# Sums of squares, and the ones that add them, in bf16; the totals of q, k and v half a step later

## The chip, the cores and the metric

The kernel runs on one core of a Trainium2 chip. The metric is the time of one execution on the device in microseconds, the median over several runs. In the text PE is TensorE, PEld its weight loads, DVE is VectorE, ACT is ScalarE, POOL is GpSimd and SP is SyncE, which issues most transfers.

## The reference

Attention with a block-causal mask, a gated two-layer network, and a routed layer of eight experts, one after the other:

```python
scores = np.where(mask, q @ k.T / 8, -1e9)      # 8 batches x 8 heads, 576 x 576, d = 64
x = softmax(scores) @ v                         # 4608 tokens x 512
x = ((x @ w1) * (x @ w2) @ w3) @ w_out          # 512 -> 1024 -> 512
# moe2: logits = x @ w_gate; greedy assignment of 4608 tokens to 8 experts of 576 places
out[mask_e] = np.maximum(x[mask_e] @ ew1[e], 0) @ ew2[e]
```

Everything is float32 in the reference.

## The kernel before, in words

A float32 operand is split into two f16 halves, a high and a low one, and a product is three f16 products (high x high, high x low, low x high). For this each operand is first scaled by a power of two that brings it to the middle of the f16 range. The power comes from a sum of squares: `ssq` (L200) lets ACT square a tile and accumulate one sum per partition in a small tile (`qm`, `vm`, `wm`, `w3m`, `wom`, `wgxm`, `wgym`), and `total` (L139) lets PE multiply a 128x128 matrix of ones with these columns, which adds them over the partitions and puts the total on each of them (L145). The product lies in one of three PSUM buffers `ab`, which the gated network also uses. DVE reads it in `pow2` (L74) and makes the power of two and its inverse with integer shifts; only the exponent of the total matters. `split` (L181) then lets ACT make the high half (L188) and DVE the low half (L183).

The work is in three stages. The first, up to about 690 us, runs attention and the gated layer together. It is cut into 64 half steps (two heads of one batch, one part of their rows), numbered h; each half step has, in this order on PE, the attention output of an earlier half step (PV, L431), the scores of the next one (S, L328 and L332, in part L392) and two units of the gated layer (L464: 12 products with `w1h`, 12 with `w2h`, then the gate product on DVE, L480, stored as g). Beside it the weights are decoded from their 64-bit form, split, and w3 and w_out multiplied together (L723, L736, `w34o`). The second stage makes the output of the network (L1152) while DVE assigns the tokens to experts. The third, from about 1054 us, runs the experts (L1344, L1362); their weights are split in `expert_w`, with totals at L1230.

Each piece of the first stage is an event with a place on a time scale of half steps: `at(p, f)` puts f at place p, `defer(d, f)` at d after the present one, and the program is written in the order of the places. `spread` looks for a free slot behind the exponentials or the gate products. Up to half step 14, some 190 us, a planner of the framework then orders all engines by its own estimate of times; from there on PE keeps the written order, and the planner orders ACT, DVE, SP and POOL alone. In the third stage PE, ACT and DVE keep the written order.

Lines that the change touches: the tile `ones` (L66) and the two masks made from it (L68, L754); `scale_v` (L218), which asks for the squares of v of a batch from place 8b - 1.4 on and for the total .55 after the last of them (L239); `qk_scale` (L264), which handles q and k of two pairs of heads as a group, with the total d1 after the second square (L274), d1 = .62 for the groups from number 6 on; and the tiles of sums elsewhere.

Of the kernel before, what the change touches and what calls it, by code (L numbers as in the profile page):

```python
# [8 lines left out]
F32 = mybir.dt.float32  # L9
F32R = mybir.dt.float32r  # L10
F16 = mybir.dt.float16
BF16 = mybir.dt.bfloat16
I32 = mybir.dt.int32
AF = mybir.ActivationFunctionType
ALU = mybir.AluOpType
# [40 lines left out]
def moe_kernel(ctx, tc, q, k, v, moe_w1, moe_w2, moe_w3, moe_w_out, w_gate, ew1, ew2, out):  # L56
    nc = tc.nc
    P = 128
# [3 lines left out]
    const = ctx.enter_context(tc.tile_pool(name="const", bufs=1))  # L62
    L = const.tile([P, NT, E], F32, name="L")
    ident = const.tile([P, P], F32, name="ident")
    i8 = const.tile([P, 8], F32, name="i8")
    ones = const.tile([P, P], F32, name="ones")  # L66
    nc.gpsimd.memset(ones, 1.0)
    nc.gpsimd.affine_select(out=ident, in_=ones, pattern=[[1, P]], compare_op=ALU.is_equal, fill=0.0,  # L68
                            base=0, channel_multiplier=-1)

    id16 = const.tile([P, P], F16, name="id16")
# [21 lines left out]
    sm = pa.enter_context(tc.tile_pool(name="sm", bufs=4))  # L93
# [21 lines left out]
    def at(p, f, *a):  # L115
        assert p >= now[0], (p, now[0])
        heapq.heappush(ev, (p, at.n, f, a))
        at.n += 1
# [3 lines left out]
    def defer(d, f, *a):  # L122
        at(now[0] + d, f, *a)
# [74 lines left out]
    sc_c, iv, sv, ivs = {}, {}, {}, {}  # L198

    def ssq(x, dst, junk):  # L200
        nc.scalar.activation(junk, x, AF.Square, accum_out=dst)

    def load_qk(g):
        n0, n1 = GROUPS[g]
# [11 lines left out]
        nc.sync.dma_start(v32, v[b])  # L216

    def scale_v(b):  # L218
        m = sm.tile([P, 3], F32, name="vm")
        vhl[4 * b] = c2.tile([P, 2, 2, 5, D], F16, name="v16", bufs=4)  # L220
        j = vhl[4 * b].rearrange("p z h j d -> p (z h j d)")

        def sq(x):
            w = min(2, 5 - 2 * x)
            ssq(v32[:, :, 2 * x:2 * x + w, :], m[:, x:x + 1],
                j[:, :H * w * D].rearrange("p (h j d) -> p h j d", h=H, j=w))

        def use(m2):
            m3 = sm.tile([P, 1], F32, name="vm3")
            nc.vector.tensor_reduce(m3, m2, axis=AX.X, op=ALU.add)  # L230
            sv[b] = pow2(sm, m3, "vp")

        for x in range(3):
            if b:
                p = spread("a", now[0] + .1 * x, sq, x)
            else:
                behind("e", sq, x)
                p = now[0] - .15
        at(p + .55, total, m, .08, use)  # L239

    def prep_v(n):
        b, hp = divmod(n, NP)
# [18 lines left out]
    pq = {}  # L261

    junk = c2.tile([P, 2, S], F16, name="junk", bufs=1)

    def qk_scale(g, d0, d1, d2):
        n0, n1 = GROUPS[g]
        w = n1 - n0

        def sq(z):
            if z == 0:  # L270
                pq[g] = sm.tile([P, 2], F32, name="qm")
            ssq(qk32[g][:, z, :w], pq[g][:, z:z + 1], junk)
            if z:
                defer(d1, total, pq[g], .08, fin)  # L274

        def fin(m2):
            T = c2.tile([P, 2, 2, 2, S], F16, name="qkT")
            s, e = pow2(sm, m2, "qp")
            c = sm.tile([P, 2], F32, name="cc")
            for z, f in enumerate((1.0, -1.0)):  # L280
                nc.vector.scalar_tensor_tensor(c[:, z:z + 1], e[:, 0:1], f * 0.125, e[:, 1:2],
                                               op0=ALU.mult, op1=ALU.mult)
            for z in range(2):
                split(T[:, z, 0, :w], T[:, z, 1, :w], qk32[g][:, z, :w], s[:, z:z + 1], .14,
                      then=lambda: end(d2), key="g5" if g == 4 else "g")
            pq[g] = s, c, T

        done = []

        def end(_):  # L290
            done.append(1)
            if len(done) < 2:
                return
            s, c, T = pq.pop(g)
            del qk32[g]
            for n in range(n0, n1):
                qkT[n] = T[:, 0, :, n - n0], T[:, 1, :, n - n0], q4[:, n % 2], c
            if g + 2 < len(GROUPS):
                load_qk(g + 2)

        if g == 4:
            defer(0, behind, "e", sq, 0)
            defer(.02, behind, "e", sq, 1)
            return
        spread("a", now[0], sq, 0)
        spread("a", now[0] + d0, sq, 1)

# [290 lines left out]
    def prep_w(f):  # L598
        w = stg_w.tile([P, 1024], F32, name="wd")
        t = [w16[n][f].rearrange("p z c f -> p z (c f)") for n in ("w1", "w2")]  # L600

        def use(m2):
            s, e = pow2(sm, m2, "wp")
            nc.vector.scalar_tensor_tensor(iw12[:, f:f + 1], e[:, 0:1], 2.0 ** 15, e[:, 1:2], op0=ALU.mult,
                                           op1=ALU.mult)
            for z in range(2):
                split(t[z][:, 0], t[z][:, 1], w[:, 512 * z:512 * z + 512], s[:, z:z + 1], .08)

        def squares():
            m = sm.tile([P, 2], F32, name="wm")  # L610
            for z in range(2):
                ssq(w[:, 512 * z:512 * z + 512], m[:, z:z + 1], t[z][:, 1])
            defer(.5, total, m, .06, use)

        decode(("w", f), w, squares)
# [4 lines left out]
    wo = {}  # L620

    def wo_chunk(c):
        if c == 0:
            es_w.close()
            wo["s2"] = es_g.enter_context(tc.tile_pool(name="stg_2", bufs=1))
            st_o = wo["stack"] = ExitStack()
            wo["pool"] = st_o.enter_context(tc.tile_pool(name="stg_o", bufs=1))
            wo["w"] = wo["pool"].tile([P, 8, 512], F32, name="wo32")
            wo["m"] = sm.tile([P, 8], F32, name="wom", bufs=1)
            wo["t"] = wo["s2"].tile([P, 8, 2, 512], F16, name="wo16", bufs=1)  # L630
            wo["g"] = wo["s2"].tile([P, 4 * E], F32, name="wg", bufs=1)
            nc.scalar.dma_start(wo["g"].rearrange("p (c e) -> p c e", e=E),
                                w_gate.rearrange("(c p) e -> p c e", p=P))
        decode(("o", c), wo["w"][:, c], lambda: ssq(wo["w"][:, c], wo["m"][:, c:c + 1], wo["t"][:, c, 1]))

    def hilo(src, k, name, then):
        m = sm.tile([P, 1], F32, name=name + "m", bufs=1)
        t = wo["s2"].tile([P, k, 2, E], F16, name=name + "h", bufs=1)
        v = src.rearrange("p (c e) -> p c e", e=E)
        ssq(v, m, t[:, :, 1])  # L640

        def use(m2):
            s, e = pow2(sm, m2, name + "p")
            split(t[:, :, 0], t[:, :, 1], v, s, .05)
            defer(.06, then, t, e)

        defer(.4, total, m, .05, use)
# [48 lines left out]
    def w3_chunk(f, h):  # L696
        if h == 0:
            wo["w3"] = wo["p3"].tile([P, 1024], F32, name="w3d", bufs=1)
        w3 = wo["w3"]

        def use(m2):
            t = wo["T", f]
            s, e = pow2(sm, m2, "w3p")
            split(t[:, 0], t[:, 1], w3, s, .12, then=lambda: wo.update({("ok", f): True}))
            fc = sm.tile([P, 2], F32, name="w3f")
            nc.vector.tensor_tensor(out=fc[:, 0:1], in0=e, in1=wo["e"], op=ALU.mult)
            nc.vector.tensor_tensor(out=fc[:, 1:2], in0=e, in1=wo["ee"], op=ALU.mult)
            wo["T", f] = t.rearrange("p z (k f) -> p z k f", f=P), fc

        def squares():  # L710
            m = sm.tile([P, 1], F32, name="w3m")
            wo["T", f] = wo["p3"].tile([P, 2, 1024], F16, name="w3h", bufs=2)
            at(spread("a", now[0], ssq, w3, m, wo["T", f][:, 1]) + .55, total, m, .06, use)

        decode(("3", f, h), w3[:, h * 512:h * 512 + 512], squares if h else lambda: None)
# [35 lines left out]
    i8b = const.tile([P, 8], F32, name="i8b")  # L751
    for x in range(4):
        t = i8b if x else i8
        nc.gpsimd.affine_select(out=t, in_=ones[:, :8], pattern=[[1, 8]], compare_op=ALU.is_equal, fill=0.0,  # L754
                                base=32 * x, channel_multiplier=-1)
        if x:
            nc.vector.tensor_tensor(out=i8, in0=i8, in1=i8b, op=ALU.add)
# [451 lines left out]
    def expert_w(e, part):  # L1209
# [3 lines left out]
        d = {}  # L1213
# [4 lines left out]

        def red(i):
            if i == 0:  # L1220
                d["m"] = cw.tile([P, 8], F32, name="em" + n, bufs=2)
                d["w"] = cw.tile([P, 2, A_, N_], F16, name="ew" + n, bufs=2)
                d["s"] = d["st"].rearrange("p c f -> p (c f)")
                d["v"] = d["w"].rearrange("p z c f -> p z (c f)")
            nc.scalar.activation(d["v"][:, 1, i * width:(i + 1) * width], d["s"][:, i * width:(i + 1) * width], AF.Square,  # L1225
                                 accum_out=d["m"][:, i:i + 1])

        def fin():
            m2 = cwp["ps"].tile([P, 512], F32, name="pe")
# [203 lines left out]
```

## Time and profile before

| | |
|---|---|
| median of 3 runs | 1443.48 us (1442.46 to 1443.8) |
| the profiled execution | 1445.88 us |
| its span in the profile | 1444.2 us |
| PE busy | 1319.5 us, 91% |
| DVE, ACT busy | 965.2 us, 952.5 us |
| mean granted clock of PE | 0.964 |

The profile is one execution. The span runs from the first to the last instruction; some 1.7 us lie around it. A row of a timeline gives start, duration, engine, line, operation and shapes, with a count where like instructions are merged, and in brackets how long the engine stood idle before it and who released it. A duration of merged products of PE runs to the end of the last one and overlaps the next row. The granted clock is 1.00 at 2.4 GHz and 0.50 at 1.2 GHz; a value between is a mean over time at the two levels.

### The profile page before, as it was taken

The numbers are of one execution on the slowest core, as the hardware profiler recorded it, in microseconds if no ns is written. First come the engines' busy times: TensorE is split into PE (matmuls) and PEld (weight loads), VectorE is DVE, ScalarE is ACT, GpSimd is POOL, SyncE is SP. The second block draws the span as 40 slices with busy tenths as digits, with TensorE's granted clock in tenths as the row PEclk, the third lists the DMA queues.
The fourth block names the chain that finished last, engine by engine and source line by source line (L and its number), as shares of the span: only waits on it lengthen the run. The fifth ranks groups of instructions, "written<-read, shape, count | busy, mean of one in ns | idle before, by whom it ended". The sixth has DMA issues, their size and how long they took to land. (4 is left out here: it accounts for less than half of the span.)

```text
span 1444.2 us, 31983 instructions
## 1 busy us (share of the span) xinstructions
PE 1319.5 (91%) x12483; PEld 909.6 (63%) x12483; DVE 965.2 (67%) x2873; ACT 952.5 (66%) x2229; POOL 114.2 (8%) x136
## 2 busy tenths in 40 slices
PE   4678889879999999999999899999889999999997
PEld 3455567657766666666676566666576566666663
DVE  7997878887988978787514677777454456354530
ACT  7896788968888888777534465455346667675641
POOL 0000000000000000010001110111032211110001
PEclk6789999999999999999999999999989999999999
DMA  9776878598977787599999978888585785665200
GB/s 291 196 180 182 196 169 176 136 194 189 190 180 157 185 190 175 137 199 246 237 286 242 224 183 199 199 212 202 148 155 141 159 199 145 174 161 155 74 30 37
DMA packets 383815, 257.47 MB, mean 178 GB/s; under 512 B 260784, under 2 KB 344752, under 8 KB 382640
## 3 DMA queue, kind: packets, MB, share of 16 engines
q1 hardware_dynamic: 370464, 213.44, 60.2%
q0 software_dynamic: 11520, 39.87, 12.5%
q10 hardware_dynamic: 1680, 2.11, 0.5%
q8 instruction: 98, 1.61, 0.5%
q14 instruction: 53, 0.43, 0.1%
HBM read 130.84 MB, written 39.86 MB: 118 GB/s over the span
## 5 line engine op out<-in xcount | busy, mean ns | idle before, releaser
L464 PE MATMUL ab<-xT,w1h 128*128 128x288 f16 x1536 | 215.6, 290 | 15.5 <-ACT a_sb L474 6.0
L464 PE MATMUL ab<-xT,w2h 128*128 128x288 f16 x1536 | 214.9, 290 | 9.6 <-ACT a_sb L474 6.7
L1344 PE MATMUL pe<-xT,ewa 128*128 128x288 f16 (+2 forms) x1728 | 193.4, 275 | 1.6 <-ACT xT L1312 0.9
L1362 PE MATMUL pe<-ewb,h 128*128 128x512 f16 (+1 forms) x960 | 189.3, 379 | 0.0
L464 PEld LDWEIGHTS <-w1h 128*128 128x128 f16 x1536 | 147.7, 100 | 60.6 <-issue 18.9
L464 PEld LDWEIGHTS <-w2h 128*128 128x128 f16 x1536 | 151.8, 99 | 53.5 <-issue 12.5
L1344 PEld LDWEIGHTS <-ewa 128*128 128x128 f16 x1728 | 158.1, 100 | 36.1 <-issue 2.0
L374 DVE SCALAR_TENSOR_TENSOR P<-E,rr,P 128x128 f16<-128x128 f32 (+4 forms) x288 | 154.5, 574 | 25.7 <-ACT P L370 22.1
L354 ACT ACTIVATE E<-S,nb,cc 128x384 f32<-128x384 f32 (+4 forms) x234 | 147.8, 640 | 2.1
L1362 PEld LDWEIGHTS <-h 128*128 128x128 f16 (+1 forms) x960 | 85.4, 101 | 98.8 <-issue 2.6
L370 ACT ACTIVATE P<-E,rr 128x384 f16<-128x384 f32 (+2 forms) x224 | 120.5, 602 | 19.2 <-issue 7.9
L1152 PE MATMUL px<-W34h,gl 128*128 128x512 f32 x288 | 120.6, 419 | 3.9 <-DMA gl<-g 3.9
L1152 PE MATMUL px<-W34h,gh 128*128 128x512 f32 x288 | 120.9, 420 | 0.8 <-ACT gh L1173 0.8
L1152 PE MATMUL px<-W34l,gh 128*128 128x512 f32 x288 | 120.3, 418 | 0.0
L431 PE MATMUL PV<-PT,v 128*64 128x128 f16 (+1 forms) x2880 | 90.1, 218 | 13.3 <-DMA PT<-P 13.0
L346 DVE TENSOR_REDUCE nb<-S 128x2 f32<-128x768 f32 (+3 forms) x128 | 100.0, 815 | 3.0 <-PE S L332 2.7
L431 PEld LDWEIGHTS <-v 128*64 128x64 f16 x2880 | 77.9, 114 | 33.1 <-issue 27.7
L1347 DVE SCALAR_TENSOR_TENSOR h<-pe,h 128x288 f16<-128x288 f32 (+2 forms) x144 | 57.8, 420 | 47.2 <-ACT h L1346 46.3
L1365 ACT ACTIVATE y<-pe,s 128x512 f32<-128x512 f32 x36 | 24.7, 687 | 95.0 <-PE pe L1362 65.8
L1302 DVE SCALAR_TENSOR_TENSOR x<-xg,xsc,x 128x512 f16<-128x512 f32 x36 | 27.1, 752 | 84.0 <-ACT x L1301 84.0
L1346 ACT ACTIVATE h<-pe 128x288 f16<-128x288 f32 (+2 forms) x144 | 52.6, 376 | 44.9 <-PE pe L1344 42.0
L1187 ACT ACTIVATE jk<-px 128x512 f16<-128x512 f32 x36 | 21.4, 595 | 89.9 <-issue 67.4
(298 smaller groups left out, 2266.9 us busy)
## 6 DMA issues: line engine op xcount, KB each, us to landing
g<-gd SPq DMA_DIRECT2D x36, 512.0 KB, 5.1
gl<-g POOLq DMA_DIRECT2D x36, 512.0 KB, 5.5
raw<-in_moe_w_dram SPq DMA_DIRECT2D x32, 512.0 KB, 4.5
esa<-in_moe_w_dram SPq DMA_DIRECT2D x8, 2048.0 KB, 8.9
esb<-in_moe_w_dram SPq DMA_DIRECT2D x8, 2048.0 KB, 11.4
gd<-g SPq DMA_DIRECT2D x56, 288.0 KB, 3.7
g<-gd SPq DMA_DIRECT2D x14, 1152.0 KB, 6.8
v<-in_v_dram SPq DMA_DIRECT2D x8, 1280.0 KB, 6.9
```

The source lines that it names most:

```text
L346: newest["m"] = nc.vector.tensor_reduce(nb[:, 0, x:x + 2], ps[:, :, o:o + N], axis=AX.X, op=ALU.max)
L354: newest["e"] = nc.scalar.activation(d["e"][:, cols[x]], pf_[:, cols[x]], AF.Exp, bias=nb[:, 1, x:x + 1], scale=c[:, 0:1], accum_out=sums[ ...
L370: nc.scalar.activation(hi, d["e"][:, cols[x]], AF.Copy, scale=r[:, 1, x:x + 1])
L374: nc.vector.scalar_tensor_tensor(lo, d["e"][:, cols[x]], r[:, 1, x:x + 1], hi, op0=ALU.mult, op1=ALU.subtract)
L431: nc.tensor.matmul(ps[hh * 64:hh * 64 + 64, c0:c0 + w], vt[:, zv, hh, j, :], s, start=z == 0 and j == 0, stop=z == 2 and j == nj - 1)
L464: nc.tensor.matmul(p[:, :288], w[:, zw, cc, :], x[:, zx, cc, c0:c0 + 288], start=first, stop=cc == 3 and zw == 1)
L1152: nc.tensor.matmul(p, gh[a][:, f], W34[b][:, f], start=f == 0 and a + b == 0, stop=f == 7 and a == 1)
L1302: nc.vector.scalar_tensor_tensor(x16[:, 1], xg[:, :DM], s, x16[:, 0], op0=ALU.mult, op1=ALU.subtract)
L1344: nc.tensor.matmul(p[:, :n], w1[:, a, cc, f * P:(f + 1) * P], t[:, 4 * b + cc, x], start=cc == 0 and a + b == 0, stop=cc == 3 and a == 1)
L1346: nc.scalar.activation(h[:, 0, f, x], p[:, :n], AF.Relu)
L1347: nc.vector.scalar_tensor_tensor(h[:, 1, f, x], p[:, :n], 0.0, h[:, 0, f, x], op0=ALU.max, op1=ALU.subtract)
L1362: nc.tensor.matmul(p[r0:r1], h[:, a, f, k_ * P + r0:k_ * P + r1], EW[e, "b"][0][:, b, f], start=f == 0 and a + b == 0, stop=f == 7 and a == 1)
```

## The change

The tiles of sums and the ones become bf16. `ident`, `i8` and `i8b`, which were made from the float32 ones, are filled by themselves first. The total of v is placed 1.2 instead of .55 after its last square for batches from 2 on, and the total of q and k .45 later for groups from 6 on. `ssq` also takes the place of the same call in `expert_w`.

```diff
-    ones = const.tile([P, P], F32, name="ones")
+    ones = const.tile([P, P], BF16, name="ones")
     nc.gpsimd.memset(ones, 1.0)
-    nc.gpsimd.affine_select(out=ident, in_=ones, pattern=[[1, P]], compare_op=ALU.is_equal, fill=0.0,
+    nc.gpsimd.memset(ident, 1.0)
+    nc.gpsimd.affine_select(out=ident, in_=ident, pattern=[[1, P]], compare_op=ALU.is_equal, fill=0.0,
                             base=0, channel_multiplier=-1)
...
     def ssq(x, dst, junk):
-        nc.scalar.activation(junk, x, AF.Square, accum_out=dst)
+        with nc.allow_low_precision(reason='the sums only choose powers of two'):
+            nc.scalar.activation(junk, x, AF.Square, accum_out=dst)
...
-        m = sm.tile([P, 3], F32, name="vm")
+        m = sm.tile([P, 3], BF16, name="vm")
...
-        at(p + .55, total, m, .08, use)
+        at(p + (.55 if b < 2 else 1.2), total, m, .08, use)
...
-                pq[g] = sm.tile([P, 2], F32, name="qm")
+                pq[g] = sm.tile([P, 2], BF16, name="qm")
             ssq(qk32[g][:, z, :w], pq[g][:, z:z + 1], junk)
             if z:
-                defer(d1, total, pq[g], .08, fin)
+                defer(d1 + (.45 if g > 5 else 0), total, pq[g], .08, fin)
...
-                d["m"] = cw.tile([P, 8], F32, name="em" + n, bufs=2)
+                d["m"] = cw.tile([P, 8], BF16, name="em" + n, bufs=2)
```

The tiles `wm`, `wom`, `w3m`, `wgxm` and `wgym` change from F32 to BF16 in the same way, and each of `i8` and `i8b` gets a fill of its own before its mask.

PE at the total of q and k of group 11, the second half of the heads of batch 5. Before (the number behind `w1h` names the block of 128 columns, 72 being the first):

```order
L328 MATMUL S<-qkT 128x128
L332 LDWEIGHTS hide
L332 MATMUL S<-low,hide 128x64
L145 MATMUL ab<-qm,ones 128x2
L464 LDWEIGHTS w1h_76
L464 MATMUL ab<-xT,w1h_76 128x288
```

And with the change (73 is the first block here, and L466 is L464 of before):

```order
L466 LDWEIGHTS w2h_85
L466 MATMUL ab<-xT,w2h_85 128x288
L146 LDWEIGHTS ones
L146 MATMUL ab<-qm,ones 128x2
L466 LDWEIGHTS w1h_78
L466 MATMUL ab<-xT,w1h_78 128x288
```

The total has moved from ahead of the first unit of its half step to between its first and its second, and it now has a load of its own in the program.

PE at the total of v of batch 5, before:

```order
L464 LDWEIGHTS w2h_83
L464 MATMUL ab<-xT,w2h_83 128x288
L145 MATMUL ab<-vm,ones 128x3
L431 LDWEIGHTS v_6046
L431 MATMUL PV<-PT_6735,v_6046 64x128
```

With the change:

```order
L466 LDWEIGHTS w2h_86
L466 MATMUL ab<-xT,w2h_86 128x288
L146 LDWEIGHTS ones
L146 MATMUL ab<-vm,ones 128x3
L433 LDWEIGHTS v_6231
L433 MATMUL PV<-PT_6967,v_6231 64x128
```

It stands ahead of the PV of the next half step now, behind one PV, one set of scores and two units more.

DVE at the low halves of q and k of the group for batch 4 (qkT<-qk), before:

```order
L480 SCALAR_TENSOR_TENSOR g<-ab,vr,a_sb 128x288
L680 TENSOR_REDUCE wg_4384<-ab 128x8
L358 TENSOR_SCALAR rr<-sums 128x1
L359 RECIPROCAL rr<-rr 128x1
L183 SCALAR_TENSOR_TENSOR qkT<-qk_3670,qp,qkT 128x1152 x2
L314 COPY q_108<-qkT 64x2x64 x2
L374 SCALAR_TENSOR_TENSOR P_120<-E,rr,P_120 128x512 x2
L374 SCALAR_TENSOR_TENSOR P_119<-E,rr,P_119 128x576
L480 SCALAR_TENSOR_TENSOR g<-ab,vr,a_sb 128x288
L437 SCALAR_TENSOR_TENSOR xT<-PV,xT 128x192
```

With the change, from the last two of these rows on:

```order
L482 SCALAR_TENSOR_TENSOR g<-ab,vr,a_sb 128x288
L439 SCALAR_TENSOR_TENSOR xT<-PV,xT 128x192
L348 TENSOR_REDUCE nb<-S 128x2
L350 TENSOR_REDUCE nb<-S 128x1
L78 TENSOR_SCALAR wgyp<-ab 128x1
L184 SCALAR_TENSOR_TENSOR qkT<-qk_3855,qp,qkT 128x1152
L80 TENSOR_SCALAR wgyp<-wgyp 128x1
L81 TENSOR_SCALAR wgyp<-wgyp 128x1
L316 COPY q_109<-qkT 64x2x64 x2
L694 SCALAR_TENSOR_TENSOR wgee<-wgyp,wop,wgxp 128x1
```

The first low half has moved behind the P halves, a gate product and the maxima of the next scores (L348, L350). The second follows behind one more gate product:

```order
L316 COPY q_109<-qkT 64x2x64 x2
L482 SCALAR_TENSOR_TENSOR g<-ab,vr,a_sb 128x288
L184 SCALAR_TENSOR_TENSOR qkT<-qk_3855,qp,qkT 128x1152
L360 TENSOR_SCALAR rr<-sums 128x2
L361 RECIPROCAL rr<-rr 128x2
```

One unit of the gated layer is left on PE between that gate product's unit and the first scores of this group.

## Rows read from the trace of the kernel before

**Rows 1.** The page's part 1, busy time and share of the span of each engine.

```profile
PE 1319.5 (91%) x12483; PEld 909.6 (63%) x12483; DVE 965.2 (67%) x2873; ACT 952.5 (66%) x2229; POOL 114.2 (8%) x136
```

**Rows 2.** Busy time by stage: PE, PEld, DVE, ACT, POOL, clock, DMA share, GB/s.

```profile
0.00:200.00 200.00, 145.66 (x1426) 99.24 (x1427) 169.74 (x425) 158.17 (x394) 1.60 (x11) 0.83 0.78 204
200.00:690.00 490.00, 454.95 (x5582) 330.44 (x5581) 402.68 (x1032) 396.83 (x985) 5.98 (x13) 0.99 0.81 181
...
1054.00:1282.00 228.00, 227.32 (x1704) 151.26 (x1704) 115.48 (x348) 144.32 (x346) 49.03 (x49) 0.99 0.70 163
```

**Rows 3.** Waits of PE, total us, times, longest: 200 to 420, then 420 to 690.

```profile
PE ab L145 <- ACT junk L201: 3.0, 2, 2.6
...
PE ab L145 <- ACT v L201: 1.9, 2, 1.3
...
PE ab L145 <- ACT w34o L728: 3.1, 2, 2.4
...
PE ab L145 <- ACT junk L201: 1.1, 2, 0.6
```

**Rows 4.** Timeline of PE around three totals, 262 to 273 us and at 448 us.

```profile
263.74 1.63 PE L464 MATMUL ab<-xT,w2h 128*128 128x288 f16 x12
266.71 0.39 PE L145 MATMUL ab<-vm,ones 128*128 128x3 f32 x2 [1.34 <-ACT v L201]
267.03 1.33 PE L431 MATMUL PV<-PT,v 128*64 128x128 f16 x54
268.29 0.82 PE L328 MATMUL S<-qkT 64*128 64x512 f16 x6
...
272.41 0.38 PE L145 MATMUL ab<-qm,ones 128*128 128x2 f32 x2 [2.56 <-ACT junk L201]
...
448.07 0.38 PE L145 MATMUL ab<-vm,ones 128*128 128x3 f32 x2 [2.38 <-ACT w34o L728]
```

**Rows 5.** Busy time in short stretches, columns as in rows 2.

```profile
445.00:450.00 5.00, 2.62 (x56) 2.22 (x56) 4.24 (x11) 4.46 (x8) 0.00 (x0) 0.87 0.79 187
450.00:455.00 5.00, 5.00 (x59) 3.29 (x54) 3.73 (x13) 2.16 (x7) 0.00 (x0) 0.78 0.89 208
...
262.00:274.00 12.00, 8.11 (x121) 6.15 (x120) 9.36 (x24) 11.20 (x23) 0.00 (x0) 1.00 0.82 201
```

**Rows 6.** Timeline of ACT behind the wait at 448 us.

```profile
450.43 0.33 ACT L442 ACTIVATE xT<-PV 128x192 f16<-128x192 f32 x1 [0.97 <-PE PV L431]
453.14 0.29 ACT L352 ACTIVATE nb<-nb,cc 128x2 f32<-128x2 f32 x1 [2.38 <-DVE nb L346]
```

**Rows 7.** Timeline of PE: eight small f16 products, and the total behind them.

```profile
337.96 0.34 PE L675 MATMUL ab<-wgxh,w3h 128*128 128x16 f16 x8
338.17 0.36 PE L145 MATMUL ab<-qm,ones 128*128 128x2 f32 x2
338.39 1.63 PE L464 MATMUL ab<-xT,w1h 128*128 128x288 f16 x12
```

**Rows 8.** Weight loads of L675: duration in ns, shortest, median, longest.

```profile
L675 PEld LDWEIGHTS <-w3h x64: 95/96/147, 304.6 to 342.0; 128*128 128x128 f16 x64
```

**Rows 9.** Timeline of PE around a total of the expert stage.

```profile
1096.55 0.28 PE L1230 MATMUL pe<-emb,ones 128*128 128x8 f32 x2
1096.69 1.46 PE L1362 MATMUL pe<-ewb,h 128*128 128x512 f16 x6
```

**Rows 10.** Timelines of DVE, and of PE at 292 us: gates, halves, scores.

```profile
264.16 0.51 DVE L480 SCALAR_TENSOR_TENSOR g<-ab,vr,a_sb 128x288 f32<-128x288 f32 x1
...
288.32 1.67 DVE L374 SCALAR_TENSOR_TENSOR P<-E,rr,P 128x384 f16<-128x384 f32 x4
...
290.65 0.50 DVE L480 SCALAR_TENSOR_TENSOR g<-ab,vr,a_sb 128x288 f32<-128x288 f32 x1
...
292.29 0.50 PE L328 MATMUL S<-qkT 64*128 64x256 f16 x6
...
344.04 2.75 DVE L183 SCALAR_TENSOR_TENSOR qkT<-qk,qp,qkT 128x1152 f16<-128x1152 f32 x2 [0.79 <-ACT qkT L188]
```

More of the change, by code (lines that the diff above doesn't have):

```diff
@@ L609, in squares @@
         def squares():
-            m = sm.tile([P, 2], F32, name="wm")
+            m = sm.tile([P, 2], BF16, name="wm")
             for z in range(2):
@@ L628, in wo_chunk @@
             wo["w"] = wo["pool"].tile([P, 8, 512], F32, name="wo32")
-            wo["m"] = sm.tile([P, 8], F32, name="wom", bufs=1)
+            wo["m"] = sm.tile([P, 8], BF16, name="wom", bufs=1)
             wo["t"] = wo["s2"].tile([P, 8, 2, 512], F16, name="wo16", bufs=1)
@@ L636, in hilo @@
     def hilo(src, k, name, then):
-        m = sm.tile([P, 1], F32, name=name + "m", bufs=1)
+        m = sm.tile([P, 1], BF16, name=name + "m", bufs=1)
         t = wo["s2"].tile([P, k, 2, E], F16, name=name + "h", bufs=1)
@@ L710, in squares @@
         def squares():
-            m = sm.tile([P, 1], F32, name="w3m")
+            m = sm.tile([P, 1], BF16, name="w3m")
             wo["T", f] = wo["p3"].tile([P, 2, 1024], F16, name="w3h", bufs=2)
@@ L753, in moe_kernel @@
         t = i8b if x else i8
-        nc.gpsimd.affine_select(out=t, in_=ones[:, :8], pattern=[[1, 8]], compare_op=ALU.is_equal, fill=0.0,
+        nc.gpsimd.memset(t, 1.0)
+        nc.gpsimd.affine_select(out=t, in_=t, pattern=[[1, 8]], compare_op=ALU.is_equal, fill=0.0,
                                 base=32 * x, channel_multiplier=-1)
@@ L1224, in red @@
                 d["v"] = d["w"].rearrange("p z c f -> p z (c f)")
-            nc.scalar.activation(d["v"][:, 1, i * width:(i + 1) * width], d["s"][:, i * width:(i + 1) * width], AF.Square,
-                                 accum_out=d["m"][:, i:i + 1])
+            ssq(d["s"][:, i * width:(i + 1) * width], d["m"][:, i:i + 1], d["v"][:, 1, i * width:(i + 1) * width])
         def fin():
```

## Prediction

> **What bounds the kernel now.** Read the share of each engine over the span first, then the same by stage. TensorE (PE) is busy 91% of the span and no other engine passes 67% [rows 1], but the stages differ [rows 2]. In the opening, 0 to 200 us, PE is busy 146 of 200 us: PE is not the bound there, ScalarE (ACT, 158) and VectorE (DVE, 170) are as full, and the planner orders all engines. From 200 to 690 us the order on PE is written by hand; PE is busy 455 of 490 us, with 35 us of waits. From 1054 us the experts run with PE busy 227 of 228 us. So time is gained by a wait of PE that goes between 200 and 690 us, or by shorter work on PE there or in the expert stage.
>
> The totals (L145) are small, but PE takes its queue in order, so a total that stands before its sums of squares are ready holds up everything behind it. The waits of PE by releaser show this: between 200 and 420 us 3.0 us for the squares of q and k, 1.9 us for those of v; from 420 to 690 us 1.1 us for q and k, and 3.1 us for a PSUM buffer that ACT must read first (w34o) [rows 3]. Together 9.1 us, in eight waits; the largest are 1.34, 2.56 and 2.38 us [rows 4]. All eight stand before totals that the change moves.
>
> **The change part by part.** *The waits, moved.* Removed by name: 9.1 us. What comes back depends on who is late next. At 262 to 274 us ACT is busy 11.2 of 12 us [rows 5]: it is the bound there, and PE, let go sooner, will meet ACT again at the next buffer. For the 4.9 us before 420 us I count a quarter, 1.2. At 448 us it is otherwise: after PE's wait ACT itself stood 0.97 us for the product of P and v, and then 2.38 us for the maxima of the next scores [rows 6]; PE was the late one, so all 2.4 us come back. For the other 1.8 us after 420 us (4.2 less 2.4) three quarters, 1.4. Sum 5.0 us; bounds 0 and 9.1.
>
> *The clock behind the longest of them.* From 445 to 455 us the granted clock was 0.87 and 0.78 of full [rows 5], that is 1.3 and 2.2 us at 1.2 instead of 2.4 GHz, half of it lost: 1.75 us. PE had stood still for 2.4 us just before. At 262 to 274 us two waits of 1.34 and 2.56 us left it at 1.00 [rows 4, 5], so it is not sure that the moved total keeps it up. I take 1.2; bounds 0 and 1.75.
>
> *One pass instead of two.* A total is now two loads of ones and two products; the next product follows 0.22 us after its first one (338.17 to 338.39) or 0.32 us (266.71 to 267.03) [rows 4, 7]. The bf16 total, one load and one product of 1 to 8 columns, does not occur. The nearest row is that of L675: eight products of 16 or fewer columns, each with its own 128x128 two-byte load, go by in 0.21 us (337.96 to 338.17), 26 ns each [rows 7]. So a total saves 0.19 to 0.29 us of PE; I take 0.24. By the order of the program 26 of the 40 totals of this helper lie after 200 us: 6.2 us of PE time. It counts in full where PE is the last to arrive and not at all where it then waits for ACT or DVE; I take half, 3.1. Bounds 0 and 6.2. The 14 in the opening I cost at nothing: they lie beside ACT and DVE [rows 2], and if PE is late there they give at most 14 x 0.29 = 4 us.
>
> Against these 26 ns speaks a rule of the Trainium skill: the page "TensorE: Matmul & The Clock Gate", section "Part 3: Packing small matmuls", says that a weight load overlaps running products only in other row groups, and these use all rows. By it each total would still pay its load. The L675 row does not agree: its loads take 96 ns each [rows 8], and eight of them do not fit one after the other into 0.21 us.
>
> *The expert stage.* 16 totals (L1230), 13 of them after 1054 us. Two passes hold the next product back 0.14 us (1096.55 to 1096.69) [rows 9]; one pass at 26 ns saves 0.11 us. PE is the bound: 13 x 0.11 = 1.4 us in full.
>
> *What comes later with the totals.* For the groups of q and k from the seventh on (ten of them) the scale, both f16 halves and the copies of q follow later. The order shows the second low half behind one more gate product, one unit (24 products of L464) ahead of the scores that need it, where both halves were two units further ahead. Two places show the new slack, taking 1.38 us for a half (2.75 us for two) [rows 10]. At 264 us the gate starts at 264.16 and takes 0.51: the half would end at 266.05, the scores start at 268.29 [rows 4, 10]: 2.2 us spare, less up to 1.3 of wait removed. At 290 us: 290.65 + 0.50 + 1.38 = 292.53, and the scores start at 292.29: 0.2 us late. The total also takes one of three PSUM buffers between two units, so the second unit needs DVE's read of it, or a gate, within its own first 12 products (1.63 us in the row at 263.74) [rows 4]. I take 0.2 us for each of ten groups, 2.0 us of loss; bounds 0 and 16, the latter 1.6 us each, if a P half of DVE stands ahead (the row at 288.32 has four in 1.67 us) [rows 10]. The total of v moves most, behind one PV, one set of scores and two units, but its scale is needed more than a half step after that: no cost.
>
> *Nothing else.* The extra fills go to GpSimd, which is busy 1.6 us of the opening's 200 [rows 2]; rounding the sums to bf16 changes no shape on ACT. But the planner, given cheaper totals, orders the opening and all of ACT and DVE anew. I see no sign in that and widen the range by 3 us each way.
>
> Sum: 5.0 + 1.2 + 3.1 + 1.4 - 2.0 = 8.7 us. The profiled execution took 1445.9 us, so 1437.2; it lies 2.4 us above the median of the three runs shown, 1443.5, so the forecast for the median is **1434.8 us**.
>
> **Rivals.** *The wait only moves on.* ACT is nearly full in most of the attention stage (397 of 490 us, DVE 403) [rows 2]; PE then meets it at the next buffer, and only the expert's 1.4 us and a sixth of the 3.1 us are left: 1.9 us, 1441.6. For it: the stretch at 262 us. Against: the one at 448 us, where ACT waited for PE. *All of it comes back*: 9.1 + 1.75 + 6.2 + 1.4 = 18.4 us and no new wait: 1425.1. For it: PE is busy 93% of 490 us. Against: ACT at 11.2 of 12. *Slower: the late halves.* DVE serves a P half before the second half of q and k in each of the ten groups, and the scores wait 1.6 us each: 16 us, against 8.7 + 2.0 = 10.7 gained: 1443.5 + 5.3 = 1448.8. It decides from (10.7 + 2.9) / 10 = 1.4 us per group on, where the loss can be measured. For it: the 0.2 us late at 290 us before any queue. Against: 2.2 us spare at 264 us. *The one pass doesn't bring its price*: the load of 96 ns stays in the open, the change then doesn't do what it says. A total saves 0.14 instead of 0.24 us, the experts' 0.01: 8.7 - 1.3 - 1.3 = 6.1 us, 1437.4; this is the result of the page's rule above.
>
> **How the numbers follow.** About 0.2% (2.9 us) is what a measurement of this kernel can tell from no change. Chances: the forecast 0.55, the wait moves on 0.17, all comes back 0.13, late halves 0.11, load in the open 0.04. Faster by over 2.9 us: 0.51 of the forecast's, all of the third and the last, 0.04 of the second: 0.72. Slower: 0.09 from the late halves and 0.01 from a bad opening: 0.10. The same: the rest, 0.18. The forecast's own range is 1428 to 1441; with all coming back at 1425 and half of the late halves the range is 1426 to 1445.
>
> **What would show it.** Right: L145 with one load and one product; no wait for "junk", "v" or "w34o" in front of it after 200 us; no fall of the clock near 445 us; 1054 to 1282 us shorter by about 0.9 us (8 totals). Wrong: new waits of PE for qkT (L328), or L464 for a_sb, g or a scale, of the same sum as the waits that went; or an opening that reaches the hand-written order some us earlier or later, which I did not cost.

## The result, and the profile after

The change took 1426.14 us, the median of 4 runs (1424.68 to 1429.15), against 1443.61 us (1442.46 to 1443.8) for the kernel before: a ratio of 0.9886, 95% interval 0.987 to 0.9902, or 17.5 us less. Measured again beside two variants (below) the ratio was 0.9878 [0.9856, 0.99]. The range of the prediction holds it by 0.1 us, which is luck: the range that the prediction gives the forecast alone, 1428 to 1441, does not hold it, and the forecast of 1434.8 us gave half of the gain. The size is that of the rival "all of it comes back" (1425.1 us), but the trace shows that not all of it came back, and that some came from a place which the forecast had set to nothing.

The profiled execution took 1425.24 us, with a span of 1423.5 us. Lines have moved by one or two: L146 is the total (L145 of before), L203 the squares (L201), L330 the scores (L328), L433 PV (L431), L466 a unit of the gated layer (L464), L476 the copy `a_sb` (L474), L482 the gate product (L480), L1232 the total of the experts (L1230). First the page's part 1, as in [rows 1]:

```profile
PE 1305.5 (92%) x12427; PEld 897.5 (63%) x12427; DVE 963.0 (68%) x2873; ACT 952.5 (67%) x2229; POOL 114.6 (8%) x141
```

PE is busy 14.0 us less; the other engines are as busy as before within 2.2 us. The same stages as in [rows 2]:

```profile
0.00:200.00 200.00, 145.93 (x1521) 100.78 (x1522) 174.31 (x435) 166.16 (x410) 2.03 (x16) 0.90 0.82 209
200.00:690.00 490.00, 461.31 (x5675) 333.35 (x5674) 405.07 (x1039) 398.00 (x992) 5.98 (x13) 0.99 0.84 188
1054.00:1282.00 228.00, 228.00 (x1544) 144.33 (x1542) 115.24 (x326) 150.79 (x356) 47.74 (x47) 1.00 0.65 165
```

In the first 200 us PE now does 95 instructions more in the same busy time (1521 against 1426), at a granted clock of 0.90 instead of 0.83: the program is further on when the hand-written order begins. From 200 to 690 us PE is busy 6.4 us more of 490. To see where time is gained, the starts of the units of the gated layer (24 products each) are read from both timelines of PE, and from that of a second profile of the change (an execution beside runs 7 and 10 below). The numbers count the pieces in which the timelines show the units; some early units stand in several pieces, so the number is 2 above the true one at unit 8 and 3 above it from unit 12 on, alike in every kernel here:

| start of | before, us | change | difference | second profile |
|---|---|---|---|---|
| unit 8 | 111.6 | 110.8 | -0.9 | +0.2 |
| unit 12 | 131.3 | 124.1 | -7.2 | -6.0 |
| unit 24 | 197.4 | 189.4 | -8.0 | -4.9 |
| unit 44 | 298.5 | 286.3 | -12.2 | -11.2 |
| unit 68 | 428.2 | 414.0 | -14.3 | -12.9 |
| unit 72 | 455.9 | 437.7 | -18.2 | -16.8 |
| unit 84 | 521.7 | 504.4 | -17.4 | -16.0 |
| unit 88 | 541.3 | 526.6 | -14.7 | -13.3 |
| unit 116 | 699.2 | 681.6 | -17.6 | -16.3 |
| first product of the experts on the chain that ended last | 1054.7 | 1036.1 | -18.6 | |
| end of the span | 1444.2 | 1423.5 | -20.7 | -19.7 |

(The profiled execution of before lies 2.3 us above its median, so the last difference is that much too large.) Three places stand out: a step of 6 us between units 8 and 12, in the opening; some 10 us from unit 24 to unit 72, where the totals were moved (12 in the second profile); and a loss of 2.7 us between units 84 and 88. Each is looked at in turn.

**The opening.** The timeline of PE there, of the kernel before, and then of the change:

```profile
122.37 1.64 PE L464 MATMUL ab<-xT,w1h 128*128 128x288 f16 x12
123.94 0.69 PE L431 MATMUL PV<-PT,v 128*64 128x128 f16 x18
127.70 2.90 PE L464 MATMUL ab<-xT,w2h 128*128 128x288 f16 x12 [3.06 <-ACT a_sb L474]
```

```profile
118.01 0.16 PE L146 MATMUL ab<-qm,ones 128*128 128x2 bf16 x1
...
121.13 1.63 PE L466 MATMUL ab<-xT,w1h 128*128 128x288 f16 x12
122.60 1.63 PE L466 MATMUL ab<-xT,w2h 128*128 128x288 f16 x12
124.07 1.63 PE L466 MATMUL ab<-xT,w1h 128*128 128x288 f16 x12
```

Before, the planner had put 18 products of PV between the two halves of a unit, PE then stood 3.06 us for a PSUM buffer, and the 12 products behind took 2.90 us instead of 1.63. With cheaper totals the planner wrote another order: these units stand in one piece, and neither the wait nor the slow clock is there.

**The moved totals.** Waits of PE at the totals and at the units, from 200 to 420 us and then from 420 to 690 us (total us, times, longest), against [rows 3]:

```profile
PE ab L146 <- ACT junk L203: 3.1, 1, 3.1
PE ab L146 <- ACT w3h L203: 1.2, 1, 1.2
```

```profile
PE ab L466 <- DVE g L482: 2.3, 1, 2.3
...
PE ab L146 <- ACT a_sb L476: 1.3, 1, 1.3
...
PE ab L146 <- ACT w3h L203: 0.7, 1, 0.7
```

The waits for v and for w34o are gone; that for the squares of q and k near 265 us stayed, 3.05 us against 2.56 us before [rows 4], and new ones came at the totals: 1.9 us for the squares of w3, 1.3 us for a PSUM buffer (a_sb), and at a unit one of 2.3 us for a gate product. The timelines of PE at the total that stands free, at the wait that stayed, and at the total of v that had stood 2.38 us at 448 us [rows 4]:

```profile
239.99 0.17 PE L146 MATMUL ab<-wom,ones 128*128 128x8 bf16 x1
240.02 1.63 PE L466 MATMUL ab<-xT,w1h 128*128 128x288 f16 x12
...
265.09 0.16 PE L146 MATMUL ab<-qm,ones 128*128 128x2 bf16 x1 [3.05 <-ACT junk L203]
265.38 3.04 PE L466 MATMUL ab<-xT,w1h 128*128 128x288 f16 x12
...
440.62 0.17 PE L146 MATMUL ab<-vm,ones 128*128 128x3 bf16 x1
440.72 1.33 PE L433 MATMUL PV<-PT,v 128*64 128x128 f16 x54
```

Ahead of a unit a total holds the next product back by 0.03 us (239.99 to 240.02), ahead of PV by 0.10 us (440.62 to 440.72); two passes took 0.22 and 0.32 us there [rows 4, 7]. So each saves some 0.2 us. The granted clock around the second and the third place, columns as in [rows 2]:

```profile
437.00:442.00 5.00, 4.76 (x86) 3.89 (x86) 3.27 (x14) 5.00 (x17) 0.00 (x0) 1.00 0.17 57
442.00:447.00 5.00, 5.00 (x60) 3.93 (x57) 5.00 (x14) 5.00 (x11) 0.00 (x0) 1.00 1.06 223
262.00:274.00 12.00, 8.19 (x112) 6.01 (x111) 9.59 (x28) 10.88 (x29) 0.00 (x0) 0.86 0.57 117
```

Where the total had cost 2.38 us and a clock of 0.87 and 0.78 [rows 5], there is no wait and the clock is full: units 68 to 72 take 3.9 us less (23.7 against 27.6). Near 265 us it is the other way round: 0.86, where it had been 1.00.

**The loss behind unit 84.** The timeline of PE:

```profile
522.72 0.17 PE L146 MATMUL ab<-vm,ones 128*128 128x3 bf16 x1
524.20 0.16 PE L146 MATMUL ab<-qm,ones 128*128 128x2 bf16 x1 [1.31 <-ACT a_sb L476]
526.62 1.89 PE L466 MATMUL ab<-xT,w1h 128*128 128x288 f16 x12 [2.26 <-DVE g L482]
```

The totals of v of batch 6 and of q and k of group 13 stand side by side. Each takes one of three PSUM buffers, the second waits for one (1.31 us), and the unit behind waits for the next (2.26 us). Behind totals that stand alone between two units there are smaller waits, here at 349 us:

```profile
348.69 0.17 PE L146 MATMUL ab<-qm,ones 128*128 128x2 bf16 x1
349.88 1.63 PE L466 MATMUL ab<-xT,w1h 128*128 128x288 f16 x12 [1.01 <-ACT a_sb L476]
```

Directly behind the ten moved totals of q and k PE stands 5.0 us in the change (2.26, 1.01, 0.84, and 0.28 or less at the others; nothing at two of them), against 0.1 us behind the same ten before. Not all of this is new: the waits of units for a_sb sum to 5.5 us from 200 to 690 us, against 5.3 before, so some of them stood at other units.

**The experts.** The chain that ended last, of before and of the change, around one total (start, duration, what):

```profile
1093.91 2.81 PE pe L1362 x13
1096.71 0.12 PE pe L1230 x2
1096.84 5.20 PE pe L1362 x24
```

```profile
1093.97 4.90 PE pe L1346 x40
1098.87 0.01 PE pe L1232
1098.88 7.37 PE pe L1346 x60
```

A total takes 0.01 us of the chain instead of 0.12. From the first product (1054.68 and 1036.05) to the chain's last piece of second-layer products (1270.05 and 1249.93) it is 215.37 us before and 213.88 us now. Of these 1.5 us the eight totals are 8 x 0.11 = 0.9; the first piece, which has no total, gives 0.6.

### The profile page after: what moved, and what is told of

It is laid out like the page before. It is cut to its first block, busy times and chain, and to the rows that moved or that the text cites. A ratio compares the mean times of both kernels' runs of the same rounds, so it can differ in the third digit from the quotient of the medians.

```text
span 1423.5 us, 31849 instructions
## 1 busy us (share of the span) xinstructions
PE 1305.5 (92%) x12427; PEld 897.5 (63%) x12427; DVE 963.0 (68%) x2873; ACT 952.5 (67%) x2229; POOL 114.6 (8%) x141
## 5 line engine op out<-in xcount | busy, mean ns | idle before, releaser
L466 PE MATMUL ab<-xT,w1h 128*128 128x288 f16 x1536 | 215.4, 289 | 12.3 <-DVE xT L439 4.0
L466 PE MATMUL ab<-xT,w2h 128*128 128x288 f16 x1536 | 212.2, 288 | 4.4 <-ACT a_sb L476 2.9
L466 PEld LDWEIGHTS <-w1h 128*128 128x128 f16 x1536 | 145.4, 99 | 68.8 <-issue 27.6
L466 PEld LDWEIGHTS <-w2h 128*128 128x128 f16 x1536 | 150.8, 99 | 46.5 <-issue 6.9
L376 DVE SCALAR_TENSOR_TENSOR P<-E,rr,P 128x128 f16<-128x128 f32 (+4 forms) x288 | 157.4, 584 | 23.7 <-ACT P L372 23.2
L372 ACT ACTIVATE P<-E,rr 128x384 f16<-128x384 f32 (+2 forms) x224 | 120.7, 605 | 16.3 <-DVE rr L361 5.7
L433 PE MATMUL PV<-PT,v 128*64 128x128 f16 (+1 forms) x2880 | 89.9, 219 | 20.9 <-DMA PT<-P 19.7
L433 PEld LDWEIGHTS <-v 128*64 128x64 f16 x2880 | 79.0, 116 | 40.9 <-issue 32.2
L348 DVE TENSOR_REDUCE nb<-S 128x2 f32<-128x768 f32 (+3 forms) x128 | 100.7, 818 | 4.6 <-PE S L334 4.2
L1173 ACT ACTIVATE gl<-g 128x1024 fp32r<-128x1024 f32 x36 | 37.9, 1056 | 60.0 <-DMA g<-gd 59.9
```

The source lines that it names most:

```text
L348: newest["m"] = nc.vector.tensor_reduce(nb[:, 0, x:x + 2], ps[:, :, o:o + N], axis=AX.X, op=ALU.max)
L372: nc.scalar.activation(hi, d["e"][:, cols[x]], AF.Copy, scale=r[:, 1, x:x + 1])
L376: nc.vector.scalar_tensor_tensor(lo, d["e"][:, cols[x]], r[:, 1, x:x + 1], hi, op0=ALU.mult, op1=ALU.subtract)
L433: nc.tensor.matmul(ps[hh * 64:hh * 64 + 64, c0:c0 + w], vt[:, zv, hh, j, :], s, start=z == 0 and j == 0, stop=z == 2 and j == nj - 1)
L466: nc.tensor.matmul(p[:, :288], w[:, zw, cc, :], x[:, zx, cc, c0:c0 + 288], start=first, stop=cc == 3 and zw == 1)
L1173: nc.scalar.activation(gh[1], g, AF.Copy, scale=-1.0)
```

## The experiments

About 9 us had not been forecast. Two theories: in A they come from the opening, whose new order the planner makes from the cheaper totals; in B from the moved totals, whose waits drag more behind them than their own length.

**1. bf16 in the old places.** The change without these two lines:

```diff
-        at(p + (.55 if b < 2 else 1.2), total, m, .08, use)
+        at(p + .55, total, m, .08, use)
...
-                defer(d1 + (.45 if g > 5 else 0), total, pq[g], .08, fin)
+                defer(d1, total, pq[g], .08, fin)
```

> The sums and the ones in bf16 everywhere, every total at its old place. Its opening (to half step 14) has the order of the changed kernel on every engine. Theory A (the opening that the planner ordered anew gives some 7 us, the moved totals some 6, the shorter products some 4): 11 us faster than the kernel before, about 1432, with the waits of PE at the totals of q, k and v back after 200 us. Theory B (the opening only shifts waits that come back later; the 17 us are those of the moved totals and what follows from them): 4 us faster, about 1439.

1438.73 us, ratio 0.9963 [0.9948, 0.9979] to 1443.84 us: 5.1 us less, nearer B's 4 us than A's 11.

**2. The two lines alone**, all sums and ones float32 as before, so the same diff as that of run 1 the other way round, on the kernel before:

> Only the later places of the totals of q, k and v, sums and ones in float32 as before. Its opening has the order of the kernel before. Theory A: 6 us faster than before, about 1437, the eight waits gone and the fall of the clock near 450 us with them. Theory B: 13 us faster, about 1430.

1433.97 us, 0.993 [0.9912, 0.9949]: 9.9 us less, between A's 6 and B's 13. Together the two give 15.0 of 17.5 us, so they nearly add. Most of the gain is the moved totals'; but this does not yet say where bf16 gets its 5 to 8 us (5.1, or 17.5 - 9.9).

**3. The change with the totals of the opening in float32** (8 of the weights, those of v of the first two batches and one group of q and k; a second matrix of ones serves them):

```diff
...
-            nc.tensor.matmul(p[:, :n], ones, m, start=True, stop=True)
+            nc.tensor.matmul(p[:, :n], ones if m.dtype == BF16 else ones32, m, start=True, stop=True)
...
-        m = sm.tile([P, 3], BF16, name="vm")
+        m = sm.tile([P, 3], F32 if b < 2 else BF16, name="vm" if b < 2 else "vmb")
...
-                pq[g] = sm.tile([P, 2], BF16, name="qm")
+                pq[g] = sm.tile([P, 2], F32 if g < 4 else BF16, name="qm" if g < 4 else "qmb")
...
-            m = sm.tile([P, 2], BF16, name="wm")
+            m = sm.tile([P, 2], F32, name="wm")
```

> The changed kernel, but the eleven totals of the opening (w1 and w2, v of batches 0 and 1, q and k of group 3) in float32 as before: the planner then orders the opening as in the kernel before, and everything behind it as in the changed one. Theory A: 7 us slower than the changed kernel, about 1433, lost before 140 us and not regained. Theory B: within 2 us of the changed kernel, about 1427.

1431.2 us, 0.991 [0.9894, 0.9927]: 12.6 us less than before, and 5.1 us more than the change by the medians, 3.5 by the two ratios. PE's order in the opening is that of the kernel before again. **4. The opposite**: before, with only these totals in bf16 (a second matrix of ones again):

```diff
...
+        if b < 2:
+            m = m.bitcast(BF16)[:, :3]
...
+                if g < 4:
+                    pq[g] = pq[g].bitcast(BF16)[:, :2]
...
-            m = sm.tile([P, 2], F32, name="wm")
+            m = sm.tile([P, 2], BF16, name="wm")
...
```

> The counterpart: only the eleven totals of the opening in bf16, everything else as before. The opening has the order of the changed kernel. Theory A: 7 us faster than before, about 1436.5, gained before 140 us and kept. Theory B: within 2 us of before, about 1443.

1446.33 us, 1.0014 [0.9997, 1.0031] to 1443.84 us, over ten runs from 1440.7 to 1451.97 us: no gain. Theory A alone falls with it. Beside run 1, on the same chip, the ratio differs by 0.0051: with the totals in their old places, one pass behind the opening gives some 7.4 us. **8. The same with the late places added**, float32 behind the opening:

```diff
-        at(p + .55, total, m, .08, use)
+        at(p + (.55 if b < 2 else 1.2), total, m, .08, use)
...
-                defer(d1, total, pq[g], .08, fin)
+                defer(d1 + (.45 if g > 5 else 0), total, pq[g], .08, fin)
```

> The changed kernel with float32 sums and ones behind the opening: the eleven totals of the opening in bf16, the later places kept. Its order on PE is that of the changed kernel. Theory A (the parts add: the opening 5 us with the late totals, the shorter products 2.7 us): 2.7 us slower than the changed kernel, about 1429. Theory B (the opening's 5 us need the shorter products behind it, since they came to nothing in e4_opening_bf16, where those were in float32): 8 us slower than the changed kernel, about 1434.

1432.86 us, 0.9903 [0.9871, 0.9936] to 1446.52 us: 13.7 us less, 3.8 us more than the late places alone gave in run 2. Against the change it is 2.5 to 3.6 us slower by the ratios (0.9886 and 0.9878), as theory A of that run had it; the 1432.86 us itself comes from a chip on which the kernel before took 1446.52 us. So the opening is worth some 4 to 5 us where the totals behind it are late, and nothing that can be measured where they are not. The 4 to 5 us are a best value: the intervals of runs 2 and 8 overlap, and those of run 3 and the change do so a little. The profiles, by the start of unit 24 and the time from there to unit 116:

| | opening's order | unit 24 against before, us | units 24 to 116, us |
|---|---|---|---|
| before | old | 0 | 501.8 |
| 1, bf16 alone | new | -7.6 | 506.9 |
| 4, opening bf16 | new | -2.3 | 508.1 |
| 2, late alone | old | -2.0 | 493.6 |
| 3, change, opening float32 | old | +1.5 | 489.4 |
| 8, opening bf16 and late | new | -5.2 | 492.5 |
| the change, two profiles | new | -8.0, -4.9 | 492.2, 490.5 |

The opening's order is what decides unit 24, within some 3 us from one profile to the next: over all thirteen profiles of this study the eight with the new order lie at -5.5 us in the mean, the five with the old one at -0.5. At unit 12 the two do not even overlap: -6.0 to -8.1 us with the new order, +0.1 to -2.5 with the old one. (The profiled execution of run 4 is its slowest, 5.6 us above its median, and tells least.) But a kernel with the old places loses it again. The waits of PE from 200 to 690 us in run 1, whose profile lies at its median:

```profile
PE S L330 <- ACT E L356: 7.0, 4, 2.3
PE PV L433 <- DMA PT<-P: 5.7, 5, 2.4
...
PE ab L146 <- ACT w34o L730: 4.1, 2, 2.6
PE ab L146 <- ACT junk L203: 2.8, 1, 2.8
```

In the kernel before, the first two were 3.0 and 3.4 us. All waits of PE in this stretch sum to 40.1 us in run 1, 34.6 before, and 28.4 in the change: PE comes earlier and waits longer, as long as the totals stand in the old places. Why run 1 is still 5.1 us faster is shown in part only: its profile is 2.5 us ahead at unit 116 and 7.2 at the end of the span (with before's profile 2.3 us above its median); where the rest is gained was not followed.

**5 and 6. One late place at a time**, float32: on the kernel before the line of v alone, then that of q and k alone.

```diff
-        at(p + .55, total, m, .08, use)
+        at(p + (.55 if b < 2 else 1.2), total, m, .08, use)
```

> Only the total of v placed later (batches 2 to 7), everything in float32, opening as before. Both late placements together gave 9.9 us (e2_late_only). Theory A (each wait of PE at a moved total counts for itself): v had 5.1 us of the waits and the fall of the clock behind the one of 2.4 us, q and k 4.1 us of which one of 2.6 us stays: 7 us faster than before, about 1437. Theory B (the gain comes from q and k, because their halves now stand behind the halves of P on ACT and DVE, so that P is turned and multiplied earlier): 3 us faster, about 1441.

```diff
-                defer(d1, total, pq[g], .08, fin)
+                defer(d1 + (.45 if g > 5 else 0), total, pq[g], .08, fin)
```

> Only the totals of q and k placed later (groups 6 to 15), everything in float32, opening as before. Theory A: 3 us faster than before, about 1441. Theory B: 7 us faster, about 1437.

1443.51 us, 0.999 [0.9968, 1.0013], and 1445.09 us, 0.999 [0.997, 1.0011], both to 1446.52 us: neither can be told from no change, and yet the two together gave 9.9 us. (By the far ends of their intervals the two would give some 9 us, so that they do not add is likely, not certain. The profiles say it too: from unit 24 to unit 116 they take 1.1 and 1.9 us less than before, run 2 takes 8.2 less.) The waits of PE at totals from 200 to 690 us tell a part of why. With v late:

```profile
PE ab L145 <- ACT junk L201: 5.8, 5, 3.4
PE ab L145 <- ACT a_sb L474: 0.9, 1, 0.9
```

With q and k late:

```profile
PE ab L145 <- ACT v L201: 11.1, 3, 5.2
PE ab L145 <- ACT a_sb L474: 1.2, 1, 1.2
```

In each the kind that was left in place now holds PE up longer: q and k 5.8 us instead of 4.1, v 11.1 us instead of 5.0 (1.9 for its squares and 3.1 for w34o). With q and k late this is enough: the waits at totals rise from 9.1 to 12.3 us. With v late they fall to 6.7 us, as in run 2, and there it is PE's other waits that stay: all of them sum to 32.3 us in run 5 and 26.9 in run 2; what holds them up was not tried. The timelines of ACT and then of PE at the longest, with q and k late:

```profile
353.63 2.00 ACT L370 ACTIVATE P<-E,rr 128x512 f16<-128x512 f32 x3
355.52 0.64 ACT L201 ACTIVATE v<-v 128x512 f16<-128x512 f32 x1
```

```profile
356.31 0.59 PE L145 MATMUL ab<-vm,ones 128*128 128x3 f32 x2 [5.16 <-ACT v L201]
356.83 1.46 PE L328 MATMUL S<-qkT 64*128 64x512 f16 x6
```

The planner, which orders ACT anew for each of these programs, put the last square of v behind three P halves; PE stood 5.16 us for it, and the six products of scores behind took 1.46 us (0.82 for the same kind in [rows 4]).

**7. The two totals side by side, parted.** The change, with v of batch 6 one unit later:

```diff
-        at(p + (.55 if b < 2 else 1.2), total, m, .08, use)
+        at(p + (.55 if b < 2 else 1.55 if b == 6 else 1.2), total, m, .08, use)
```

> The changed kernel with the total of v of batch 6 one unit later. In the changed kernel this total and one of q and k stand side by side at 523 us and PE waits 1.3 and 2.3 us there; the order differs in this one place on PE. Theory A (two totals side by side hold two of the three PSUM buffers until DVE reads them): both waits go, 3 us faster than the changed kernel, about 1423. Theory B (DVE and ACT are behind there anyway, and PE meets them at the next buffer): within 1 us of the changed kernel, about 1426.

1426.77 us, 0.9862 [0.9836, 0.9888], measured without the change beside it. So it was run again with the change, and with one step more: **run 10** also moves the total that stands 3.05 us near 265 us.

```diff
-        at(p + (.55 if b < 2 else 1.55 if b == 6 else 1.2), total, m, .08, use)
+        at(p + (.55 if b < 2 else 1.55 if b in (3, 6) else 1.2), total, m, .08, use)
...
-                defer(d1 + (.45 if g > 5 else 0), total, pq[g], .08, fin)
+                defer(d1 + (.8 if g == 7 else .45 if g > 5 else 0), total, pq[g], .08, fin)
```

> The change itself once more, with the next two on one chip. If the first result stands: ratio to before 0.9886, 1426 to 1428 us. If the 1.5 us that it loses in units 84 to 92 by the two totals side by side, and the 3.1 us wait of the total of q and k near 265 us, depend on the draw, they are missing in this trace; I expect both again, since the order of PE is written by hand there.

> Theory A (side by side totals share the three PSUM buffers and cost PE 1.3 + 2.3 us there, all of it on the path): 3 us below the change itself on the same chip, ratio to before lower by 0.002. Theory B (that wait is only the place where PE meets DVE, the time is lost again a few units on): within 1 us of the change.

> As the one before, and the total of q and k for the second half of the heads of batch 3, where PE stands 3.05 us near 265 us for the squares, placed one unit later (.8 instead of .45), with v of batch 3 one unit later too (1.55). Theory A (PE is the bound there once the total is late enough): the 3 us come back, 3 us below the one before. Theory B (ACT is full there, 11.2 of 12 us before: the wait moves to the next unit, for a_sb or for the scores' exponentials): the wait at the total goes below 1.5 us, waits of PE for a_sb, E or qkT rise by as much in 265 to 290 us, and the time is within 1 us of the one before.

On one chip: the change 1426.67 us, ratio 0.9878 [0.9856, 0.99]; with v of batch 6 apart 1423.14 us, 0.9849 [0.9828, 0.9871]; with group 7 later too 1423.88 us, 0.9853 [0.9833, 0.9874]. The parted totals give 3.5 us more (theory A of that run), and this version is the fastest of the study with 20.9 us less than before. The intervals of the change and of it overlap a little; the profiles agree on the place: units 84 to 88 take 22.2 us in both of the change's, 19.8 in both of the variant's, 19.5 before. So the place itself gives 2.4 us of the 3.5. Its timeline of PE there:

```profile
523.08 0.16 PE L146 MATMUL ab<-qm,ones 128*128 128x2 bf16 x1 [1.02 <-ACT junk L203]
525.70 1.63 PE L466 MATMUL ab<-xT,w2h 128*128 128x288 f16 x12 [0.70 <-ACT a_sb L476]
527.16 0.17 PE L146 MATMUL ab<-vm,ones 128*128 128x3 bf16 x1
```

1.7 us of waits are left of 3.6. Run 10 brings nothing beyond it (theory B): the wait at the total is gone, and others stand around it, in the timeline of PE:

```profile
265.44 1.63 PE L466 MATMUL ab<-xT,w2h 128*128 128x288 f16 x12 [1.86 <-ACT a_sb L476]
266.91 0.17 PE L146 MATMUL ab<-qm,ones 128*128 128x2 bf16 x1
267.92 1.11 PE L433 MATMUL PV<-PT,v 128*64 128x128 f16 x46 [0.49 <-DMA PT<-P]
...
271.18 0.66 PE L330 MATMUL S<-qkT 64*128 64x384 f16 x6 [1.58 <-ACT E L356]
```

1.86 + 0.49 + 1.58 = 3.9 us in place of 3.05. From 255 to 295 us all waits of PE sum to 8.3 us, against 7.5 in the second run 7. Here PE meets ACT at the next step, as the rival "the wait only moves on" had it.

## Why the prediction was right, and why only by half

The forecast was 8.7 us; 17.5 us were measured. The runs give each term its own size:

| term | forecast, us | measured, us | from |
|---|---|---|---|
| moved waits, clock, less the late halves | 5.0 + 1.2 - 2.0 = 4.2 | 9.9 | run 2 |
| one pass behind the opening, experts included | 3.1 + 1.4 = 4.5 | 2.8 | run 3 against run 2 |
| the opening | 0, within 3 | 5.1 (3.5 by the ratios) | the change against run 3 |
| sum | 8.7 | 17.7 | |

The three are steps of one path from before to the change, so they sum up to it (0.2 us above 17.5, as the kernel before took 1443.84 us beside runs 2 and 3). The intervals of neighbouring steps overlap, and that the terms hang on each other runs 4 to 6 show: along another path, from run 4 to run 1, one pass gave 7.4 us and not 2.8.

**The opening** is the first step that failed: "The 14 in the opening I cost at nothing: they lie beside ACT and DVE", and of the planner "I see no sign in that". The totals' own passes may well be hidden there, but the planner's order is made from their price, and the trace of before had the place that another order could mend: a wait of 3.06 us for a PSUM buffer with a unit at half clock behind it, 4.3 us at 125 us, cut out by the new order. Whether the whole 5 us is the order or partly the shorter totals was not separated. That the gain shows only with the late places (runs 4 and 8) no step of the prediction had foreseen either.

**The moved waits** are the second: "For the 4.9 us before 420 us I count a quarter, 1.2". In the profile of run 2, where nothing but the places differs, PE goes from -2.0 us at unit 24 to -8.4 at unit 68, 428 us in the kernel before: 6.4 us, more than the waits by name in that stretch. The quarter was read from ACT's 11.2 busy us of 12 at 262 to 274 us. That place is indeed held by ACT, as run 10 shows, and its wait stayed; but the verdict was then laid on all the waits before 420 us. Nor do the named waits bound the gain: at the totals the waits fell only from 9.1 to 6.7 us in run 2, those of PE in the stretch altogether from 34.6 to 26.9. The term for 448 us was right: 2.4 us of wait and 1.2 of clock forecast, units 68 to 72 shorter by 3.9 us.

**The late halves** cost nothing at the scores: no score after 200 us waits for qkT in the change. The other half of that paragraph, the PSUM buffer that a total takes between two units, came true: behind the ten totals and at the one that meets another PE stands 5.0 + 1.3 = 6.3 us, against 2.0 forecast for all ten. How much of that is lost is shown for the one place alone where two totals meet: 2.4 us by the profiles and 3.5 by the medians of the runs with v of batch 6 apart, so this place by itself took what was forecast for all.

**One pass** was priced nearly rightly (0.2 us for 0.24) and, on this path, counted too high. The pitch of 0.03 us ahead of units and of the experts' products agrees with the 26 ns taken from [rows 7]; the 0.10 us ahead of PV and of scores was not in the forecast. The Trainium skill's page "TensorE: Matmul & The Clock Gate", section "Part 3: Packing small matmuls", lists that a load overlaps running products only in other row groups, though the same section also lets a load into the background weight buffer run ahead. By the list a total would show its load, which takes 98 ns in the median here. Ahead of units the trace speaks against it once more; ahead of PV and of scores, where the pitch is as long as a load, it does not decide. In the experts the eight totals give the 0.9 us named. Behind the opening the 26 totals come to 2.8 us with the experts, so 1.3 to 1.9 us without them (2.8 - 1.5 or 2.8 - 0.9): a fifth to a third of 6.2 us rather than half.

Of what was to show it right: one load and one product, the clock at 448 us and the experts' 0.9 us held; "no wait for junk" did not, the one near 265 us stayed. Of what was to show it wrong, waits for g and a_sb came, with 3.6 us at one place, and the opening was earlier. The rival "all of it comes back" met the number by two errors that cancel: 18.4 us of named waits, clock and passes, of which some 12.7 came, and 5 us of the opening that it did not have.

## What to carry to other kernels

Where several kinds of events can each hold up a queue, moving one kind alone may show nothing, since the engine then stands before the next kind: judge a set of moves together before one of them is dropped. Where a scheduler orders part of the program by its own estimate of times, a cheaper instruction is also a new order; look in the trace of before for waits and slow clock in the part that it orders, since these are what another order can give or take. And after moving events later, look for two that now meet and share buffers: one such place in the table of places was worth 2.4 us by the profiles and 3.5 by the medians.

## What the runs showed that was not expected

The clock behind one and the same wait. Near 265 us eight profiles show PE standing 3.05 us (3.04 to 3.35) at the total of q and k with much the same work around it. Behind it the next 24 products ran at full clock in four (run 3, run 7, run 8 and the second profile of the change: 1.63 us for 12), and at half clock for a part of them in the other four (the change 3.04 us, run 2 3.04, the second profile of run 7 2.91, run 5 3.09 for its second 12). In the kernel before a wait of 2.56 us there left the clock at 1.00. Over 262 to 282 us the granted clock was 0.91 in one profile of the change and 1.00 in the other. So a wait of this length puts some 1.5 to 1.7 us at stake here (the 24 products took 4.4 to 4.6 us instead of 2.9), and whether they are lost differs between two executions of one program; a forecast can give it a chance, not a value.
